# Group order, in-place weight rounding and queue choice in a one-core Strassen mixture-of-experts kernel

## The chip, the cores and the metric

The kernel runs on one core of one Trainium2 chip. The metric is the device time of one execution in microseconds. The median of three runs of the kernel before is 2360.71 us (2359.41 to 2364.94).

## What is computed

One token block `x` of 2048 rows and 512 columns goes through two branches, and a gate mixes them row by row:

```
g = sigmoid((x * gate_w).sum(-1))                      # one number per row
a = linear attention of x: 32 heads of 16, phi(t) = (t > 0 ? t + 1 : exp(t)) + 1e-6 on q and k,
    num = phi(q) @ (phi(k)^T v), den = phi(q) . sum(phi(k)), a = (num / den) @ wo
b = sum over 8 experts e of  softmax(x @ w_gate)[e] * (silu(x @ w1[e]) @ w2[e])   # all 8 chosen
out = g * a + (1 - g) * b
```

`w1[e]` is 512 x 1792 and `w2[e]` 1792 x 512. Everything is float32 in and out.

## The kernel before, in words

A float32 product is made of three passes on numbers rounded to the TensorE's 32-bit format: high x high, high x low, low x high (`mm3`, lines 57 to 60; `high` is a ScalarE copy that rounds, `low` a VectorE subtraction of what the rounding lost). All large products use a seven-product scheme on 2 x 2 blocks, so that each group of blocks has seven products P1 to P7, and sums and differences of blocks are made on VectorE.

The program is one order written out by hand, engine by engine, without a scheduler. It has two stages.

*Keys* (`keys`): projections for k, the gates' logits and `yT = x^T phi(k)`, and the running sum `pks` of phi(k), which GpSimd's queue adds up by 16 accumulating DMAs. At its very start four pieces of `x` and four of the weights `wk` are loaded in turn from SyncE's queue (SP); nine matmuls on zeros (`idle`) run on TensorE (PE) meanwhile. The last row tiles of this stage also prepare group 0 of the next (`prep(0, ...)`).

*Experts* (`experts`): a loop over ticks `u`. A *group* is a pair of hidden-column blocks: seven ticks, in six of which its first-layer ("up") products run, six matmuls of 128 x 512 per product; the seventh product runs in the second tick of the next group. `m.groups` is the order of the groups. Seven groups make one expert for one half of the rows (`X[h][e]`); two groups (`A[h]`, q = 0 and 1) make the attention queries of a half. The hidden activation of an expert group is one Silu on ScalarE (ACT); that of a query group is `phi`: Exp and Relu on ACT, one operation on VectorE (DVE), and a store to `pqd` by GpSimd's queue. Beside the products of group g, `prep(g + 1, step)` makes the operands of group g + 1 from raw weights (`rm`, loaded by `load(g + 2)` at the group's first tick): roundings on ACT, remainders and block sums on DVE. For groups of the first half (`both`) it also makes the second layer's weights, stores them to DRAM (`w2stash`, from tiles `ws`, and while `m.spare` is set, `wx`), and `load_w2` brings them back in pairs when they are needed. Query groups have no second layer in `prep`: it is lighter there.

The second-layer ("down") products start at u = 58 (`LAG`): from there each tick has one up product and one down product (`tick`). So the first 58 ticks have half the PE work per tick, and the same work on ACT, DVE and the DMA queues per group. In the kernel before, the query groups of the first half stand at places 0 and 4 of `m.groups`.

Small steps sit at fixed ticks: `state` (u = 5, the matmuls `kv`), `fold` (u = 7 to 10, matmuls `wp`), `normaliser` (u = 4, matmuls `z` that read `pks`), `gate_rows` (u = 65, two transposes into a bank of tag `a`, and 17 small stores that `load_wb` reads back at u = 74). PSUM banks: `a` two, `b` and `c` one each, `p` four for the down products. A group uses bank `a` for P1, for product 3 of the list, for product 5 and, in the next group, product 6; each of these waits until the step before has been read: by the copies on ACT (L663) or the additions on DVE (L668, L674). ACT, DVE and SP each work strictly in order.

At the end `columns(dt, ...)` transposes the last 512 rows, copies each of four column blocks out of PSUM in two halves and stores each half from SP; `dt` 2 and 3 in the last two ticks, 0 and 1 after the loop.

Of the kernel before, what the change touches and what calls it, by code (L numbers as in the profile page):

```python
# [11 lines left out]
F32R = mybir.dt.float32r  # L12
# [4 lines left out]
P = 128  # L17
# [7 lines left out]
TB = 512  # L25
NTB = S // TB
NTT = TB // P
# [3 lines left out]
G = (256, 266)  # L31
NPAIR = NF // 2
HALF = 2 * P
NHT = NT // 2
# [3 lines left out]
def f32(ap):  # L38
    return ap.bitcast(F32)


@with_exitstack
def gated_mix_kernel(ctx: ExitStack, tc: tile.TileContext, xT, x, wk, wv, wqkv_q, wo, wm, out):
    nc = tc.nc
    PS = bass.MemoryType.PSUM

    const = ctx.enter_context(tc.tile_pool(name="const", bufs=1))
    xpool = ctx.enter_context(tc.tile_pool(name="xpool", bufs=14))
    w1p = ctx.enter_context(tc.tile_pool(name="w1p", bufs=1))
    psum = ctx.enter_context(tc.tile_pool(name="psum", bufs=1, space=PS))  # L50
    dram = ctx.enter_context(tc.tile_pool(name="dram", bufs=1, space=bass.MemoryType.DRAM))
    ctx.enter_context(tc.manual_schedule())

    m = SimpleNamespace(nc=nc, tc=tc, const=const, xpool=xpool, w1p=w1p, psum=psum, v=nc.vector,
                        xT=xT, x=x, wk=wk, wv=wv, wq=wqkv_q, wo=wo, wm=wm, out=out)

    def mm3(ps, wh, wlo, xh, xl, start, stop):
        nc.tensor.matmul(ps, wh, xh, start=start, stop=False, skip_group_check=True)  # L58
        nc.tensor.matmul(ps, wh, xl, start=False, stop=False, skip_group_check=True)  # L59
        nc.tensor.matmul(ps, wlo, xh, start=False, stop=stop, skip_group_check=True)  # L60

    def act_copy(dst, src, scale=1.0, bias=0.0):
        nc.scalar.activation(dst, src, AF.Copy, scale=scale, bias=bias)  # L63

    def ps_tile(name, tag, bufs=None):
        return psum.tile([P, TB], F32, name=name, tag=tag, bufs=bufs or {"a": 2, "b": 1, "c": 1, "dn": 4}[tag])

    m.mm3, m.act_copy, m.ps_tile = mm3, act_copy, ps_tile


    def phi(dst, src):
        nc.scalar.activation(dst, src, AF.Exp)
        nc.scalar.activation(src, src, AF.Relu)
        nc.vector.scalar_tensor_tensor(dst, dst, 1.0, src, op0=ALU.min, op1=ALU.add)

    def eps_high(h, d):
        act_copy(h, d, bias=EPS)

    def eps_low(lo, d, h):
        nc.vector.scalar_tensor_tensor(lo, d, EPS, f32(h), op0=ALU.add, op1=ALU.subtract)  # L80

    m.phi, m.eps_high, m.eps_low = phi, eps_high, eps_low
    m.ident = const.tile([P, P], F32, name="ident")


    def x_tile(name, tag="x"):
        return xpool.tile([P, 2, TB], F32R, name=name, tag=tag, bufs=14 if tag == "x" else 2)

    m.x_tile = x_tile
    m.XO = [[None] * 7, [None] * 7]  # L90
    m.xstash = dram.tile([7, 2, P, 2 * TB], F32, name="xstash")
    m.w2stash = [dram.tile([P, 2, D], F32, name=f"w2stash{i}") for i in range(7 * (E * NPAIR + 2) // 2)]
    m.wgtd = dram.tile([E + 1, S], F32, name="wgtd")
    m.acct = dram.tile([2, 2, KT, P, TB], F32, name="acct")
    m.pqd = dram.tile([2, 2, KT, P, TB], F32, name="pqd")
    m.wpd = [dram.tile([P, D], F32, name=f"wpd{c}") for c in range(KT)]
    m.zcd = dram.tile([P, KT * 2 * NH], F32, name="zcd")
    m.spd = dram.tile([P, KT * P], F32, name="spd")

    X = [[SimpleNamespace(e=e, h=h, n=NPAIR) for e in range(E)] for h in range(2)]
    A = m.A = [SimpleNamespace(e=E, h=h, n=2) for h in range(2)]
    M = E // 2

    m.parts = [*X[0], *X[1][:M], A[0], *X[1][M:], A[1]]
    at = 0
    for part in m.parts:
        part.t0, at = at, at + 7 * part.n
    m.NTICK = at  # L110
    m.groups = [(part, q) for part in (*X[0], *X[1][:M], A[1], *X[1][M:]) for q in range(part.n)]

    m.groups.insert(0, (A[0], 0))
    m.groups.insert(4, (A[0], 1))
    m.NG = len(m.groups)
    for part in m.parts:
        part.gs = [g for g, (p, _) in enumerate(m.groups) if p is part]
    m.G1 = X[1][0].gs[0]

    m.beside = [*X[1][:2], *X[1][M:M + 2]]  # L120

    misc = ExitStack()
    m.misc = misc.enter_context(tc.tile_pool(name="misc", bufs=1, side="right"))


    def pad(pool):
        nc.gpsimd.memset(pool.tile([P, 24], F32, name="pad", tag="pad", bufs=1), 0.0)

    m.pad = pad
    weights(m)  # L130
    keys(m)
    experts(m, misc)

def weights(m):
# [50 lines left out]
    def prep(g, step):  # L187
# [25 lines left out]
        def low2(n, src, *prods):  # L213
            if both:
                w = ws.pop((g, n))
                v.tensor_sub(two(w, 1), src, f32(two(w, 0)))  # L216
                for half, prod in enumerate(prods):
                    stash(part, q, prod, w[:, :, half * HALF:(half + 1) * HALF])

        def block(i, j):  # L220
            return r[:, i, j] if both else r[:, i, j, 0]

        if step == 0:
            ops[g] = [None] * 7
            high(0, r[:, 0, :, 0], (0, 0), (2, HALF))
        elif step == 1:
            low(0, r[:, 0, :, 0])
            o = o_tile(f"o{g}_1", "oh", 2, HALF)
            act_copy(o[:, 0], r[:, 1, 1, 0])
            ops[g][6] = o, 0  # L230
            if both:
                act_copy(ws_tile(0)[:, 0, :HALF], r[:, 0, 0, 1])
            high2(1, r[:, :, 1, 1] if both else None)
        elif step == 2:
            o = ops[g][6][0]
            v.tensor_sub(o[:, 1], r[:, 1, 1, 0], f32(o[:, 0]))
            if both:
                w = ws.pop((g, 0))
                v.tensor_sub(w[:, 1, :HALF], r[:, 0, 0, 1], f32(w[:, 0, :HALF]))
                stash(part, q, "P1", w[:, :, :HALF])  # L240
        elif step == 3:
            low2(1, r[:, :, 1, 1] if both else None, "P2", "P4")
            v.tensor_add(block(1, 1), block(1, 0), block(1, 1))
            v.tensor_sub(block(1, 0), block(0, 0), block(1, 0))
        elif step == 4:
            v.tensor_sub(block(0, 0), block(1, 1), block(0, 0))
            v.tensor_sub(block(0, 1), block(0, 1), block(0, 0))
            high(2, r[:, 1, :, 0], (5, 0), (1, HALF))
        elif step == 5:
            low(5, r[:, 1, :, 0])  # L250
            high2(2, r[:, :, 0, 1] if both else None)
        elif step == 6:
            low2(2, r[:, :, 0, 1] if both else None, "P6", "P7")
            high(3, r[:, 0, :, 0], (3, 0), (4, HALF))
            high2(3, r[:, :, 1, 1] if both else None)
        else:
            low(3, r[:, 0, :, 0])
            low2(3, r[:, :, 1, 1] if both else None, "P3", "P5")
# [50 lines left out]
def keys(m):  # L309
# [76 lines left out]
    r1 = [hl_tile(f"r1{i}", F32) for i in range(2)]  # L386
    for k in range(KT):
        nc.sync.dma_start(x0[:, k, :], m.xT[0][:, k * TB:(k + 1) * TB])
        nc.sync.dma_start(r0[:, k, :], m.wk[:, k * G[0]:(k + 1) * G[0]])
    for i in range(2):  # L390
        at = KT * G[0] + 2 * i * G[1]
        nc.sync.dma_start(r1[i][:, :, :G[1]], m.wk[:, at:at + 2 * G[1]].rearrange("p (k f) -> p k f", k=2))
# [175 lines left out]
def experts(m, misc):  # L568
# [171 lines left out]

    w2s = {}

    ENDS = (NU + 12 - LAG) // 2

    def load_w2(i):
# [276 lines left out]
    def columns(dt, tag):  # L1022
        ps = ps_tile(f"oc{dt}", tag)
        for tt in range(NTT):
            nc.tensor.matmul(ps[:, tt * P:(tt + 1) * P], sums[1, dt, 1][:, tt * P:(tt + 1) * P], m.ident,
                             start=tt == 0, stop=True, is_transpose=True, skip_group_check=True)
        r = r_tile(f"oc{dt}")
        for i in range(2):
            c = slice(i * HALF, (i + 1) * HALF)
            if i and dt < 2:  # L1030
                v.tensor_copy(r[:, c], ps[:, c])
            else:
                act_copy(r[:, c], ps[:, c])
            at = (NHT + NTT + 2 * i) * P
            nc.sync.dma_start(m.out[at:at + 2 * P, dt * P:(dt + 1) * P].rearrange("(t p) d -> p t d", p=P),
                              r[:, c].rearrange("p (t d) -> p t d", d=P))


    AHEAD = {}
# [16 lines left out]

    drain()
    touch()
    loaded = highs = lows = 0
    ROWS0 = 105  # L1060
    for u in range(LAG + NTICK):
        n = u - LAG
# [52 lines left out]
            fold(u - 7)  # L1115
        if u in (0, 2, 59, 60, 62):
            gates((0, 2, 59, 60, 62).index(u))
        if u == 4:
            normaliser()
        if u == 65:  # L1120
            gate_rows()
        if u == 17:
            misc.close()
            m.w2p = ctx.enter_context(tc.tile_pool(name="w2p", bufs=1, side="right", reuse_waits="tile"))
        if u == 74:
# [3 lines left out]
        while loaded < END // 2 and loaded <= (n + (5 if u < NU + 8 else 9)) // 2:  # L1129
            load_w2(loaded)  # L1130
            loaded += 1
            if loaded == 3:
                m.pad(m.w2p)
        if g == m.G1 - 1 and k != 1:
            x_next(max(k - 1, 0))
        if g == m.G1 and k == 1:
# [56 lines left out]
```

## Time and profile before

| | |
|---|---|
| profiled execution | 2360.7 us, span 2359.0 us |
| median of three runs | 2360.71 us |
| PE busy | 2339.7 us (99%), 10492 matmuls |
| DVE busy | 1822.9 us (77%) |
| ACT busy | 1412.0 us (60%) |
| granted clock, mean | 0.998 |
| moved by DMA | 514.81 MB, mean 218 GB/s |

The span is what the trace covers; the execution's own time is 1.7 us more. Times below are microseconds from the span's start. In timeline rows the columns are start, duration, engine, line, operation, tiles, shape and count, and in brackets the engine's idle time just before and what ended it. A matmul's recorded duration overlaps the next one's.

### The profile page before, as it was taken

The page shows a single profiled execution, that of the slowest core. Times are in us where ns is not written, and L with a number is a line of the kernel's source. Part 1 is how long each engine was busy: PE and PEld are TensorE (multiplying, and loading weights), DVE is VectorE, ACT ScalarE, POOL GpSimd, SP SyncE. Part 2 cuts the span into 40 slices and gives each one's busy share as a digit, 9 for nine tenths or more (in the row PEclk, how much of TensorE's full clock was granted, in tenths as well). Part 3 has the DMA queues.
Part 4 walks back from the last instruction along what each step waited for, and adds up shares of the span by engine and source line. Part 5 has one row for each costly group of instructions (what it writes and reads, how often), then busy time and mean ns, then how long its engine had stood idle before and what let it go on. Part 6 is the DMA issues. An engine that isn't in the chain of part 4 may idle for free.

```text
span 2359.0 us, 31410 instructions
## 1 busy us (share of the span) xinstructions
PE 2339.7 (99%) x10492; PEld 1936.0 (82%) x10492; DVE 1822.9 (77%) x3103; ACT 1412.0 (60%) x2659; POOL 160.1 (7%) x222
## 2 busy tenths in 40 slices
PE   9999999999999999999999999999999999999998
PEld 8877888888888888888888888888888888888887
DVE  6788888888888888888677767776677777766666
ACT  6576666666666666666555555555565655555553
POOL 2101000000000000000000000000011000000101
PEclk9999999999999999999999999999999999999999
DMA  7778898888888898888845454654456645555566
GB/s 234 237 261 278 266 288 260 264 265 276 266 262 276 262 283 262 263 270 267 285 143 173 148 178 145 182 187 147 147 172 190 186 147 176 161 165 166 164 223 202
DMA packets 300593, 514.81 MB, mean 218 GB/s; under 512 B 24448, under 2 KB 195472, under 8 KB 300048
## 3 DMA queue, kind: packets, MB, share of 16 engines
q1 hardware_dynamic: 277088, 466.33, 59.6%
q0 software_dynamic: 23344, 46.49, 10.6%
q8 instruction: 82, 1.34, 0.2%
q14 instruction: 79, 0.65, 0.1%
HBM read 345.00 MB, written 163.52 MB: 216 GB/s over the span
## 4 chain that ended last, share of the span: by engine, by line
PE 93%; DVE 3%; DMA 2%; ACT 1%; issue 1%; SPq 0%; DVEq 0%; ACTq 0%
PE p L58 15%; PE p L60 15%; PE p L59 15%; PE a L58 8%; PE a L60 8%; PE a L59 8%; PE c L58 4%; PE c L60 4%; PE c L59 4%; PE b L60 2%; PE b L58 2%; PE b L59 2%; PE g L441 2%; DVE ho L738 1%; PE y L58 1%
## 5 line engine op out<-in xcount | busy, mean ns | idle before, releaser
L58 PE MATMUL p<-ho,w 128*128 128x512 f32 x1620 | 631.6, 390 | 1.8 <-ACT p L63 0.8
L60 PE MATMUL p<-ho,w 128*128 128x512 f32 x1620 | 630.3, 389 | 0.0
L59 PE MATMUL p<-ho,w 128*128 128x512 f32 x1620 | 630.3, 389 | 0.0
L738 DVE TENSOR_TENSOR ho<-s,ho 128x512 fp32r<-128x512 f32 x784 | 536.5, 685 | 47.8 <-ACT ho L63 45.9
L63 ACT ACTIVATE ho<-s 128x512 fp32r<-128x512 f32 x784 | 486.3, 621 | 14.0 <-PE p L60 8.0
L58 PEld LDWEIGHTS p<-ho,w 128*128 128x128 f32 x1620 | 304.1, 188 | 68.1 <-ACT p L63 2.9
L60 PEld LDWEIGHTS p<-ho,w 128*128 128x128 f32 x1620 | 304.1, 188 | 63.4
L59 PEld LDWEIGHTS p<-ho,w 128*128 128x128 f32 x1620 | 304.2, 188 | 62.9
L606 ACT ACTIVATE s<-s 128x512 f32<-128x512 f32 x224 | 141.3, 631 | 266.4 <-DVE s L668 198.8
L63 ACT ACTIVATE o<-rm 128x512 fp32r<-128x512 f32 x240 | 136.5, 569 | 83.5 <-PE a L60 60.8
L668 DVE TENSOR_TENSOR s<-c,s 128x512 f32<-128x512 f32 x116 | 80.1, 690 | 136.5 <-PE c L60 130.7
L63 ACT ACTIVATE o<-rs 128x512 fp32r<-128x512 f32 x224 | 127.3, 568 | 65.6 <-PE a L60 59.9
L63 ACT ACTIVATE ws<-rm 128x512 fp32r<-128x512 f32 x206 | 116.0, 571 | 64.9 <-DMA w2stash<-ws 56.3
L674 DVE TENSOR_TENSOR s<-a,s 128x512 f32<-128x512 f32 x116 | 80.0, 690 | 71.1 <-PE a L60 70.8
L606 ACT ACTIVATE s<-b 128x512 f32<-128x512 f32 x112 | 67.0, 599 | 113.3 <-PE b L60 100.9
L202 DVE TENSOR_TENSOR o<-rm,o 128x512 fp32r<-128x512 f32 x180 | 123.2, 685 | 3.9 <-ACT o L63 3.8
L63 ACT ACTIVATE s<-a 128x512 f32<-128x512 f32 x116 | 69.1, 596 | 90.7 <-PE a L60 89.8
L202 DVE TENSOR_TENSOR o<-rs,o 128x512 fp32r<-128x512 f32 x168 | 114.8, 683 | 7.7 <-ACT o L63 7.3
L216 DVE TENSOR_TENSOR ws<-rm,ws 128x512 fp32r<-128x512 f32 x156 | 106.8, 684 | 5.1 <-ACT ws L63 5.0
L63 ACT ACTIVATE s<-c 128x512 f32<-128x512 f32 x116 | 69.0, 595 | 25.6 <-PE c L60 25.6
L784 POOL DMA_DIRECT2D acct<-c x30 | 25.6, 852 | 801.4 <-DVE c L778 630.5
L63 ACT ACTIVATE b<-a 128x512 f32<-128x512 f32 x116 | 67.1, 579 | 21.4 <-PE a L60 21.1
(319 smaller groups left out, 4543.5 us busy)
## 6 DMA issues: line engine op xcount, KB each, us to landing
w<-w2stash SPq DMA_DIRECT2D x406, 512.0 KB, 4.0
w2stash<-ws SPq DMA_DIRECT2D x362, 256.0 KB, 4.3
rm<-wm SPq DMA_DIRECT2D x228, 256.0 KB, 5.1
rs<-wm SPq DMA_DIRECT2D x108, 256.0 KB, 4.0
wb<-wgtd SPq DMA_DIRECT2D x16, 512.0 KB, 5.3
w2stash<-wx SPq DMA_DIRECT2D x30, 256.0 KB, 4.2
acct<-c POOLq DMA_DIRECT2D x30, 256.0 KB, 5.4
acct<-d POOLq DMA_DIRECT2D x30, 256.0 KB, 5.4
```

Of the source, the lines that this page charges most:

```text
L58: nc.tensor.matmul(ps, wh, xh, start=start, stop=False, skip_group_check=True)
L59: nc.tensor.matmul(ps, wh, xl, start=False, stop=False, skip_group_check=True)
L60: nc.tensor.matmul(ps, wlo, xh, start=False, stop=stop, skip_group_check=True)
L63: nc.scalar.activation(dst, src, AF.Copy, scale=scale, bias=bias)
L202: v.tensor_sub(two(o, 1), src, f32(two(o, 0)))
L216: v.tensor_sub(two(w, 1), src, f32(two(w, 0)))
L441: nc.tensor.matmul(ps, xk((0, 0, 1)[j], tb, k, tt * P, (tt + 1) * P), gw[g][:, (0, 1, 0)[j], k, :], start=(k == 0 and j == 0), stop=(k == ...
L606: nc.scalar.activation(dst, src, AF.Silu)
L668: v.tensor_add(sn[g, 2], bank[g, "c"], sn[g, 2])
L674: v.tensor_add(sn[g, 3], bank[g, "a"], sn[g, 3])
L738: v.tensor_sub(h[1], s, f32(h[0]))
L784: nc.gpsimd.dma_start(m.acct[part.h, j, dt], s, accum_op=ALU.add)
```

## The change

Five edits. (1) The first half's two query groups are groups 0 and 1. (2) For the first six groups of the first expert the weights of P1 are rounded straight into the tiles from which the down products read them (`first_w2`), so they take no `ws` or `wx` tile and the first three `load_w2` fall away; the store to DRAM stays, since the second half reads it. For this the pool of those tiles opens at u = 7, not 17. (3) `normaliser` runs at u = 7, not 4, and `gate_rows` at u = 67, not 65. (4) At the start the four loads of `wk` are issued from ACT, those of `x` from SP. (5) At the end `columns` copies a whole block on ACT and stores it with one DMA for `dt` 0, 2 and 3; for `dt` 1 ACT and DVE copy a half each, and ACT and SP issue one store each.

```
-    m.groups = [(part, q) for part in (*X[0], *X[1][:M], A[1], *X[1][M:]) for q in range(part.n)]
-    m.groups.insert(0, (A[0], 0))
-    m.groups.insert(4, (A[0], 1))
+    m.groups = [(part, q) for part in (A[0], *X[0], *X[1][:M], A[1], *X[1][M:]) for q in range(part.n)]
...
+        begin = part is m.parts[0] and q < 6
+
+        def first(c):
+            return m.first_w2(q)[:, c] if begin else ws[g, 0][:, c, :HALF]
...
+            if both and not begin:
+                ws_tile(0)
             if both:
-                act_copy(ws_tile(0)[:, 0, :HALF], r[:, 0, 0, 1])
+                act_copy(first(0), r[:, 0, 0, 1])
...
-                w = ws.pop((g, 0))
-                v.tensor_sub(w[:, 1, :HALF], r[:, 0, 0, 1], f32(w[:, 0, :HALF]))
-                stash(part, q, "P1", w[:, :, :HALF])
+                v.tensor_sub(first(1), r[:, 0, 0, 1], f32(first(0)))
+                stash(part, q, "P1", m.first_w2(q) if begin else ws.pop((g, 0))[:, :, :HALF])
...
-        nc.sync.dma_start(r0[:, k, :], m.wk[:, k * G[0]:(k + 1) * G[0]])
+        nc.scalar.dma_start(r0[:, k, :], m.wk[:, k * G[0]:(k + 1) * G[0]])
...
+    def first_w2(q):
+        if q // 2 not in w2s:
+            w2s[q // 2] = m.w2p.tile([P, 2, 2, HALF], F32R, name=f"w2{q // 2}", tag="w2", bufs=3)
+            if q == 4:
+                m.pad(m.w2p)
+        return w2s[q // 2][:, q % 2]
...
-        for i in range(2):
+        at = (NHT + NTT) * P
+        rows = m.out[at:at + TB, dt * P:(dt + 1) * P].rearrange("(t p) d -> p t d", p=P)
+        if dt != 1:
+            act_copy(r, ps)
+            nc.sync.dma_start(rows, r.rearrange("p (t d) -> p t d", d=P))
+            return
+        for i, (copy, queue) in enumerate(((act_copy, nc.scalar), (v.tensor_copy, nc.sync))):
             c = slice(i * HALF, (i + 1) * HALF)
-            if i and dt < 2:
-                v.tensor_copy(r[:, c], ps[:, c])
-            else:
-                act_copy(r[:, c], ps[:, c])
-            at = (NHT + NTT + 2 * i) * P
-            nc.sync.dma_start(m.out[at:at + 2 * P, dt * P:(dt + 1) * P].rearrange("(t p) d -> p t d", p=P),
-                              r[:, c].rearrange("p (t d) -> p t d", d=P))
+            copy(r[:, c], ps[:, c])
+            queue.dma_start(rows[:, 2 * i:2 * i + 2], r[:, c].rearrange("p (t d) -> p t d", d=P))
...
-    loaded = highs = lows = 0
+    loaded, highs, lows = 3, 0, 0
...
-        if u == 4:
+        if u == 67:
+            gate_rows()
+        if u == 7:
             normaliser()
-        if u == 65:
-            gate_rows()
-        if u == 17:
             misc.close()
             m.w2p = ctx.enter_context(tc.tile_pool(name="w2p", bufs=1, side="right", reuse_waits="tile"))
...
-            if loaded == 3:
-                m.pad(m.w2p)
```

More of the change, by code (lines that the diff above doesn't have):

```diff
@@ L741, in experts @@
     w2s = {}
+    def first_w2(q):
[4 more added lines that the diff above has]
+        return w2s[q // 2][:, q % 2]
+    m.first_w2 = first_w2
     ENDS = (NU + 12 - LAG) // 2
```

## The prediction

> **What bounds the kernel now.** I read the page first, then a table of stretches, then who PE waited for, then the timeline at each of those waits.
>
> ```profile
> span 2359.0 us, 31410 instructions
> PE 2339.7 (99%) x10492; PEld 1936.0 (82%) x10492; DVE 1822.9 (77%) x3103; ACT 1412.0 (60%) x2659; POOL 160.1 (7%) x222
> ...
> 150.00:175.00 25.00, 21.17 (x84) 16.33 (x84) 19.33 (x32) 19.62 (x35) 2.28 (x5) 0.93 0.73 243
> 175.00:200.00 25.00, 22.57 (x97) 17.72 (x96) 21.54 (x37) 17.97 (x37) 0.00 (x0) 1.00 0.92 296
> 600.00:1130.00 530.00, 530.00 (x2340) 439.01 (x2339) 450.05 (x744) 340.62 (x643) 26.20 (x31) 1.00 0.87 268
> ...
> PE a L58 <- DVE s L674: 3.5, 2, 2.5
> PE z L870 <- DMA pks<-pk: 3.0, 1, 3.0
> PE wt L906 <- ACT s L606: 0.9, 1, 0.9
> ```
>
> PE is the bound: it idles 2359.0 - 2339.7 = 19.3 us of the span. Columns of the stretches: length, then PE, PEld, DVE, ACT, POOL busy, granted clock, DMA share, GB/s. In the long middle a matmul starts every 530 / 2340 = 0.226 us and nothing stands idle, so a tick's up product is 6 x 0.226 = 1.36 us. The change takes out no matmul; it can only take out idle and slow time at the start, around 97 to 220 us, and at the end. The rows of waits give us in total, times and longest. The idle lies in a few places: 25.00 - 21.17 = 3.8 and 25.00 - 22.57 = 2.4 between 150 and 200, 3.0 at `z`, the rest at the two ends.
>
> **The wait of `z` (edit 3).**
>
> ```profile
> 106.11 1.32 PE L870 MATMUL z<-ones,pks 128*128 128x32 f32 x8 [2.98 <-DMA pks<-pk]
> 107.24 0.77 PE L58 MATMUL c<-x11h,o 128*128 128x512 f32 x1
> 109.95 3.83 PE L854 MATMUL kv<-yT,wv 128*128 128x128 f32 x32
> 116.37 1.02 PE L861 MATMUL wp<-wo,kvt 128*128 128x512 f32 x2
> 106.11:109.95 3.84, 3.84 (x15) 3.26 (x16) 1.41 (x4) 0.00 (x0) 0.00 (x0) 0.58 1.06 390
> ...
> 98.85 7.12 DMA pks<-pk
> L840 SPq DMA_DIRECT2D wv<-wv x4: 340/443/928, 92.2 to 98.9; - x4
> L842 SPq DMA_DIRECT2D wo<-wo x4: 430/550/1191, 99.3 to 101.0; - x4
> ...
> wv<-wv SPq DMA_DIRECT2D x4, 256.0 KB, 5.1
> wo<-wo SPq DMA_DIRECT2D x4, 256.0 KB, 7.0
> ```
>
> PE stands 2.98 us because the last of the 16 additions to `pks` lands at 98.85 + 7.12 = 105.97. Behind the wait the granted clock is 0.58 until 109.95; in that time run `z` and the six matmuls of one up product, which last from the end of `z` (107.24, the start of its first matmul) to the start of `kv` (109.95): 2.71 us where 1.36 is usual. The price of the wait is 2.98 + 1.35 = 4.3 us.
>
> At u = 7 `z` comes after the products of u = 5, 6 and 7, `kv` and one `fold`. From 102.97 (106.11 - 2.98 is 103.13, less the 0.16 by which a matmul's record outlasts its slot): product to 104.33, `kv` (3.6) to 107.96, products to 110.7, `fold` 1.0, so `z` starts near 111.6, 5.6 us after `pks` has landed, and it is moved past no load on SP. What is late next: `kv` comes 5.6 us earlier and needs `wv`, whose last load was issued at 98.9 and lands 5.1 us later by the median, 104.0; `kv` starts at 104.3 and needs that quarter last, at 107. `fold` (two matmuls, 1.02) needs `wo` (issued by 101.0, 7.0 us, 108.0) at 110.7. Both are covered, by 2 to 3 us. DVE queues `zf` behind `z`: what waits behind it is a `low` for group 2, due 14 us later. The saving is 4.3; 3.5 if one of them comes late by a microsecond, 4.6 if `z` itself, too, ran slowly.
>
> **The second query group (edit 1).**
>
> ```profile
> 152.27 1.28 ACT L72 ACT_TABLE_LOAD   x1
> 155.73 0.50 PE L58 MATMUL a<-t5h,o 128*128 128x512 f32 x1 [0.29 <-ACT s L63]
> 157.22 0.69 DVE L668 TENSOR_TENSOR s<-c,s 128x512 f32<-128x512 f32 x1
> 161.22 0.70 PE L58 MATMUL a<-t6h,o 128*128 128x512 f32 x1 [2.48 <-DVE s L674]
> 161.22:165.65 4.43, 4.43 (x13) 3.50 (x13) 2.50 (x4) 3.81 (x8) 0.54 (x1) 0.61 0.75 261
> 170.95 0.50 PE L58 MATMUL a<-t5h,o 128*128 128x512 f32 x1 [1.06 <-ACT s L63]
> ```
>
> Here group 4 is a query group. Its sixth product may not touch bank `a` before DVE's L674 has read it, and on DVE L674 stands behind the `phi` of the block before: L668, Exp, Relu, `phi`'s DVE step, one `low`, L674. From the start of L668 to the matmul that is 161.22 - 157.22 = 4.0 us. Product 4 had ended by 155.73 - 0.29 = 155.44, so L668 ran 1.8 us late, after the Exp table load of 1.28. Price of the place: 0.29 + 2.48 idle, then 12 matmuls in 4.43 instead of 2.72 (clock 0.61), 1.7; and at 170.95, behind the return to the Silu table, 1.06. In all 5.5 us.
>
> In the changed kernel this group is number 1, behind another query group: no Exp load, and the load of the Silu table comes at u = 17. The chain of 4.0 us stays; L668 can start about 0.2 after product 4 (the 0.16 of a matmul's record, rounded up), and two products (2.72) lie between it and the matmul: a wait of 4.2 - 2.7 = 1.5 at u = 15. At u = 20 the wait of 1.06 comes again, and more: ACT and DVE lost the 1.7 us in which PE ran slowly and they caught up. How much of the 1.7 comes back as idle no row shows, between nothing (1.06) and all (2.8); I take 2.0, about half. So 3.5 remain and 2.0 are saved. At best (waits wholly covered by the four folds and `z` that now lie in group 1) 5.5 are saved; at worst the clock falls behind both waits, 2 x 1.7 more: 1.4 lost. The Trainium skill (TensorE: Matmul & The Clock Gate, section What's actually happening) halves the clock after at least one idle window of about 3.4 us; by that rule neither new wait would cost clock, and the trace differs, with half clock behind 2.48 us.
>
> **Weights rounded in place (edit 2).** Three loads of 512 KB fall away near 190 to 206, where DMA share is up to 0.99, and six `wx` tiles. PE idles 11.55 - 10.11 = 1.4 us in the group that starts at 182.00:
>
> ```profile
> 182.00:193.55 11.55, 10.11 (x43) 7.73 (x42) 8.98 (x15) 7.04 (x15) 0.00 (x0) 1.00 0.99 321
> 187.57 2.73 SPq L183 DMA_DIRECT2D w2stash<-ws  x3
> 190.48 0.38 SPq L754 DMA_DIRECT2D w<-w2stash  x1
> 193.46 0.63 ACT L63 ACTIVATE ws<-rm 128x512 fp32r<-128x512 f32 x1 [1.46 <-DMA w2stash<-ws]
> ```
>
> ACT stands there for a `ws` tile whose store is still out; this is the first expert's seventh group, which the edit leaves as it is, and the store was issued at 187.57, ahead of the first of the three loads (190.48). So I count 0, with 0.5 gained or lost as ends. The rounding itself takes the same operations.
>
> **`gate_rows` later (edit 3).** The row `PE wt` shows 0.9: the transposes need bank `a`, still being read from the tick before. At u = 67 that read is over: 0.9 saved, 0 if ACT is as late there.
>
> ```profile
> L913 POOL DMA_DIRECT2D wgtd<-wt x1: 507/507/507, 231.4 to 231.4; - x1
> ...
> DMA to landing us min/median/max: 2.5/4.1/5.4
> ...
> 243.35 0.33 SPq L772 DMA_DIRECT2D wb<-wgtd  x1
> ```
>
> Its 17 stores on GpSimd's queue move by two ticks, 4 x 1.36 = 5.4 us; the last, issued at 231.4, lands by 236.8 at the latest, so after the move by 242.2, and `load_wb` reads them at 243.35. A microsecond of cover stays; without it SP would hold its stores and loads back by as much, ahead of weights that are loaded two ticks early, so 0.
>
> **First loads and last stores (edits 4, 5).**
>
> ```profile
> 0.82 1.28 ACT L63 ACT_TABLE_LOAD   x1 [0.82 <-PEq L1185]
> 3.85 0.63 ACT L63 ACTIVATE x00h<-x 128x512 fp32r<-128x512 f32 x1 [1.75 <-DMA x<-xT]
> 1.28 0.42 SPq L389 DMA_DIRECT2D r<-wk  x1
> 6.92 1.21 PE L441 MATMUL g<-g,x00h 128*128 128x256 f32 x8 [0.38 <-ACT g L63]
> 8.90 1.21 PE L441 MATMUL g<-g,x01h 128*128 128x256 f32 x8 [0.18 <-ACT g L63]
> ...
> 2353.41 3.07 SPq L1035 DMA_DIRECT2D y<-oc  x6
> 2354.00:2355.00 1.00, 0.00 (x0) 0.00 (x0) 0.56 (x2) 0.05 (x1) 0.00 (x0) 1.00 1.00 318
> ```
>
> PE's idle at the start that loads can remove is 0.38 + 0.18 = 0.56. Four issues on ACT at 0.42 (SP's price; none from ACT is in the trace) push the table load from 0.82 to 2.5, its end to 3.8, just where `x` lands. I take 0.4 saved; ends 0.6 saved, 0.5 lost if an issue costs ACT more.
>
> At the end six issues at 0.5 become three on SP and one on ACT; by issue alone 1.4 us. But while they run the DMA engines are fully busy (share 1.00 from 2354 to 2355), and the bytes stay. I take 0.5; ends 1.4 saved and 0.4 lost. A rule that speaks against both edits: the Trainium skill (DMA: Bandwidth & Descriptors, section Issuing engines are not separate DMA queues) says that issuing from several engines saves only issue time. The busy share of the tail agrees with it.
>
> **The sum:** 0.4 + 4.3 + 2.0 + 0 + 0.9 + 0.5 = 8.1 us. The profiled execution took 2360.7, the median of the runs is the same: 2352.6.
>
> **Rivals.** *Two queues bring nothing.* Only the two middle gains and `gate_rows` stay: 7.2, so 2353.5. For: the full DMA engines of the tail. Chance 0.10.
>
> *Clock falls again.* The waits at u = 15 and 20 are near what cost clock before (2.48; 1.06 did not). Both with half clock: 2352.6 + 3.4 = 2356.0, about on the border of 0.2%. Chance 0.13.
>
> *The change doesn't do what it says.* `z` no longer waits, but `kv`, `fold` or group 2's operands do, by as much, since the loads of u = 0 and the `wv` and `wo` are all moved toward PE by 4 us with DMA share near 1: 2352.6 + 4.3 = 2356.9. Against: 2 to 3 us of cover. Chance 0.10.
>
> *Slower.* Groups 1 to 7 now all prepare full expert groups; before, a light one lay between.
>
> ```profile
> 172.44:182.00 9.56, 9.56 (x43) 7.85 (x42) 9.13 (x16) 7.66 (x16) 0.00 (x0) 1.00 0.91 287
> 137.59:147.11 9.52, 9.52 (x43) 7.88 (x42) 6.83 (x13) 6.42 (x13) 0.00 (x0) 1.00 0.82 262
> ```
>
> A full group needs 9.13 us of DVE in 9.56, a light one 6.83: nothing is left to catch up in, and raw weights land only as their group begins. If each of the six groups before the last paid what the group of 182.00 pays, 11.55 - 9.52 = 2.0, that is 12.2, and with one fall of the clock (1.7) 2366.5. It decides once a full group's DVE time passes 9.52. Against: the group of 172.44 runs without idle at 9.13. Chance 0.05.
>
> **How the numbers follow.** The forecast has 0.62. 0.2% is 4.7 us, about what a measurement tells from no change; the border is 2356.0. Faster: 0.62 + 0.10 + half of 0.13 = 0.79; same: the other half and 0.10, 0.16; slower 0.05. Low end: every term at its best, 0.6 + 4.6 + 5.5 + 0.5 + 0.9 + 1.4 = 13.5, 2347.2. High end: 2357.5, past the two cases near 2356 and 2357; the slow rival stays out.
>
> **What would show it.** Right: no idle before `z`, which stands after `wp`; PE idle of 1 to 2 us on DVE L674 at u = 15 and on ACT at u = 20, with the granted clock whole; about 1.4 us of idle, as before, while the first expert's seventh group is prepared; no idle at `wt`; the last store landing about 0.5 us closer behind the last transpose. Wrong: idle at `kv` or `wp`; half clock after 110; idle in every group between 140 and 185; a tail shorter by over 1 us.

## The result and the profile after

The changed kernel took 2351.48 us by the median of six runs (2350.17 to 2352.28); the kernel before took 2361.51 us on the same chip (six runs, 2357.91 to 2368.32). The ratio is 0.9954, 95% interval 0.9939 to 0.9969: 10.0 us faster, where 8.1 was forecast. The profiled execution, the shortest of the six, took 2350.17 us, 10.5 less than the one before it. Lines of code are those of the changed kernel from here on: L674 of before is now L678, L668 is L672, L870 is L883.

The head of the page, and the rows of who PE waited for (us in total, times, longest):

```profile
span 2348.5 us, 31397 instructions
PE 2335.1 (99%) x10492; PEld 1933.3 (82%) x10492; DVE 1820.5 (78%) x3102; ACT 1408.8 (60%) x2655; POOL 158.1 (7%) x222
...
PE a L58 <- ACT s L63: 2.6, 2, 1.9
PE a L58 <- DVE s L678: 2.0, 2, 1.4
```

PE's idle is 2348.5 - 2335.1 = 13.4 us where it was 19.3, and there is no row for `z` or `wt` any more. The span shrank by more than the 5.9 us of idle, mainly because PE also worked at half clock after two of the old waits, and that is booked as busy. So I compare when the same up products start:

```
first matmul of up tick   0        12       42       58       79       last matmul ends   span ends
before                 97.53   125.35   172.44   197.57   256.12      2353.62            2358.95
after                  96.65   119.64   164.45   189.13   246.53      2343.42            2348.47
gained on the way       0.88     4.83     2.28     0.45     1.15         0.61               0.28
```

The timeline of PE at the places of the prediction (start, duration, operation, and in brackets the idle before):

```profile
103.45 3.73 PE L867 MATMUL kv<-yT,wv 128*128 128x128 f32 x32
...
109.76 1.02 PE L874 MATMUL wp<-wo,kvt 128*128 128x512 f32 x2
110.61 0.97 PE L883 MATMUL z<-ones,pks 128*128 128x32 f32 x8
...
125.29 0.50 PE L58 MATMUL a<-t6h,o 128*128 128x512 f32 x1 [1.39 <-DVE s L678]
...
134.34 0.50 PE L58 MATMUL a<-t5h,o 128*128 128x512 f32 x1 [1.92 <-ACT s L63]
...
216.36 0.27 PE L919 MATMUL wt<-ident,gates 128*128 128x128 f32 x1
...
134.34:138.00 3.66, 3.66 (x16) 2.99 (x17) 3.64 (x7) 2.64 (x6) 0.00 (x0) 1.00 1.02 369
```

`kv`, `wp`, `z` and `wt` start with no idle before them. The second query group still waits twice, at u = 15 and u = 20, and the stretch behind the longer wait runs 16 matmuls in 3.66 us at clock 1.00 (the two columns after POOL's are the granted clock and the DMA share); before, the stretch behind the 2.48 ran 13 in 4.43 us at 0.61.

The two ends, as timeline rows:

```profile
0.82 1.87 ACTq L393 DMA_DIRECT2D r<-wk  x4
2.72 1.28 ACT L63 ACT_TABLE_LOAD   x1 [2.72 <-issue]
4.55 1.36 ACT L63 ACTIVATE x00h<-x 128x512 fp32r<-128x512 f32 x2 [0.55 <-DMA x<-xT]
5.24 1.22 PE L445 MATMUL g<-g,x00h 128*128 128x256 f32 x8
6.29 0.64 PE L445 MATMUL g<-g,x00l 128*128 128x256 f32 x4
6.78 1.12 PE L445 MATMUL g<-g,x00h 128*128 128x256 f32 x8
...
2341.95 1.47 PE L1038 MATMUL oc<-ident,tl 128*128 128x128 f32 x12
2343.26 0.98 SPq L1045 DMA_DIRECT2D y<-oc  x2
2344.03 0.40 ACTq L1050 DMA_DIRECT2D y<-oc  x1
2344.48 0.37 SPq L1050 DMA_DIRECT2D y<-oc  x1
2345.00:2346.00 1.00, 0.00 (x0) 0.00 (x0) 0.00 (x0) 0.00 (x0) 0.00 (x0) 0.99 0.97 285
```

At the start the two waits of `g` (0.38 and 0.18) are gone. At the end the last issue is over at 2344.48 + 0.37 = 2344.85, 1.43 us behind the last transpose (2.86 before), yet the span ends 5.05 us behind it (5.33 before). From 2345 to 2346 the DMA engines are busy 0.97 of the time although nothing is issued any more.

### The profile page after: what moved, and what is told of

The parts are those of the page before. It is cut to its first block, busy times and chain, and to the rows that moved or that the text cites. A ratio compares the mean times of both kernels' runs of the same rounds, so it can differ in the third digit from the quotient of the medians.

```text
span 2348.5 us, 31397 instructions
## 1 busy us (share of the span) xinstructions
PE 2335.1 (99%) x10492; PEld 1933.3 (82%) x10492; DVE 1820.5 (78%) x3102; ACT 1408.8 (60%) x2655; POOL 158.1 (7%) x222
## 4 chain that ended last, share of the span: by engine, by line
PE 96%; DVE 2%; ACT 1%; issue 1%; DMA 0%; SPq 0%; DVEq 0%; ACTq 0%
PE p L58 15%; PE p L60 15%; PE p L59 15%; PE a L58 9%; PE a L60 9%; PE a L59 9%; PE c L60 4%; PE c L58 4%; PE c L59 4%; PE b L60 2%; PE b L58 2%; PE b L59 2%; PE g L445 2%; PE y L58 1%; PE y L60 1%; PE y L59 1%
## 5 line engine op out<-in xcount | busy, mean ns | idle before, releaser
L672 DVE TENSOR_TENSOR s<-c,s 128x512 f32<-128x512 f32 x116 | 80.0, 690 | 133.3 <-PE c L60 129.2
L678 DVE TENSOR_TENSOR s<-a,s 128x512 f32<-128x512 f32 x116 | 80.0, 690 | 70.8 <-PE a L60 70.3
```

The costliest lines, as they stand in the source:

```text
L672: v.tensor_add(sn[g, 2], bank[g, "c"], sn[g, 2])
L678: v.tensor_add(sn[g, 3], bank[g, "a"], sn[g, 3])
```

## The experiments

Each was measured beside the kernel before on the same chip. The medians of before were 2361.04 for the first three experiments and the old loads and stores, 2362.02 for the three edits, the clock, the half stores and `gate_rows`, 2360.68 for the last two kernels. A tick's time below is that of the first matmul of its up product; where a figure is given for several kernels, each has one trace.

**The normaliser's place alone.** The kernel before, with

```
-        if u == 4:
+        if u == 7:
             normaliser()
```

> The kernel before with one change: normaliser at u = 7. Theory (each wait has its own price): the wait of z (2.98 us idle, then 1.35 us lost at the low clock) goes, some 4.5 us less, about 2356.2; the waits of the second query group stay as before (0.3 + 2.5 + 1.1 us idle, one stretch of low clock). Rival (the pause is needed): ACT, DVE and the DMA queues caught up in it, and the waits between 130 and 200 us grow by as much, so about 2360.5.

2354.97 us (2354.47 to 2355.58), ratio 0.9975 [0.9965, 0.9985]. Its tick 12 starts at 120.27, 22.99 after tick 0 (97.28); before, that took 27.82. The difference, 4.83, is what the whole change gains there. The second query group keeps both of its old prices:

```profile
156.15 0.78 PE L58 MATMUL a<-t6h,o 128*128 128x512 f32 x1 [2.43 <-DVE s L674]
165.97 0.50 PE L58 MATMUL a<-t5h,o 128*128 128x512 f32 x1 [1.15 <-ACT s L63]
156.15:160.00 3.85, 3.85 (x10) 3.09 (x11) 2.50 (x4) 3.14 (x7) 0.54 (x1) 0.56 0.74 254
```

Ten matmuls in 3.85 us at clock 0.56 behind the 2.43. The term of `z` is confirmed, as a whole and by itself. The medians differ by more, 6.1; in the traces 0.8 of the rest lies behind u = 79, where this edit does nothing.

**The groups' order alone.** The kernel before, with

```
-    m.groups = [(part, q) for part in (*X[0], ...
-    m.groups.insert(0, (A[0], 0))
-    m.groups.insert(4, (A[0], 1))
+    m.groups = [(part, q) for part in (A[0], *X[0], ...
```

> The kernel before with one change: both query groups of the first half in front. Theory: z still waits 3 us for pks and the clock falls; at u = 15 and 20 PE idles about 1.4 and 2.0 us at full clock in place of 0.3 + 2.5 + 1.1 us and a low clock, so 2 us less, about 2358.5. Rival (the order carries the whole gain, since an all-query start leaves the queues free): z's wait shrinks too, 5 us or more less, 2355.5 or below.

2355.26 us (ten runs, 2352.99 to 2364.39), ratio 0.9983 [0.9972, 0.9994]. Here my theory failed and its rival held. The wait of `z` at u = 4 was to stay, and in the profiled run it is gone. PE's row of `z`, the row of SP's loads of group 1's raw weights, and what the trace says of the last addition to `pks` (its issue, then issue to landing):

```profile
102.73 0.98 PE L868 MATMUL z<-ones,pks 128*128 128x32 f32 x8
87.18 4.45 SPq L167 DMA_DIRECT2D rm<-wq  x4
L459 POOL DMA_DIRECT2D pks<-pk x1: 852/852/852, 97.2 to 97.2; - x1
...
DMA to landing us min/median/max: 4.7/4.7/4.7
```

The last addition is issued at 97.2 and lands at 101.9, 0.8 ahead of `z`; before, it was issued at 98.85 and landed at 105.97. Group 1 is now a query group, and its raw load has no second-layer half: four loads of query weights instead of a full `rm`. So the order and the normaliser's place each remove this wait, and their gains don't add. With the old order the addition landed at 106.0 and 105.7 in two traces, with the new one between 101.9 and 105.3 in eight of ten. That the smaller load is why is likely, not shown. And the landing isn't firm. In the changed kernel's profiled run the same last addition went out much later:

```profile
L465 POOL DMA_DIRECT2D pks<-pk x1: 852/852/852, 103.3 to 103.3; - x1
...
DMA to landing us min/median/max: 7.1/7.1/7.1
```

It landed at 110.4, 0.2 us ahead of `z` at 110.61; in one more of the ten it landed as late, at 110.2. With the order alone `z` stands 102.73 - 97.29 = 5.44 us behind the start of tick 0. By that, as an estimate, `z` at u = 4 would have waited 8.3 us in the changed kernel's trace, 7.4 in the other late one, 0.3 to 2.9 in five and not at all in three. Three of the ten runs of the order alone took 2360.0 to 2364.4 us, the other seven 2353.0 to 2356.3; a late `pks` in those three would fit, but only one run was profiled.

**The changed kernel without the rounding in place.**

```
-        begin = part is m.parts[0] and q < 6
+        begin = False
...
-    loaded, highs, lows = 3, 0, 0
+    loaded, highs, lows = 0, 0, 0
... (and the pad of the pool behind the third load, as before)
```

> The changed kernel without the rounding in place: the six P1 weights go through wx tiles again and the first three loads of second-layer weights are back. Theory: 0 to 0.5 us more (2351.5 to 2352), all of it between u = 53 and 60. Rival (the three loads of 512 KB fall where the DMA engines are full and hold the stores of ws back): 2 us more or over, 2353.5 or above, as longer idle of PE between u = 54 and 60.

2352.68 us (2351.70 to 2353.24), ratio 0.9962 [0.9948, 0.9977], 1.2 us above the changed kernel's median: more than the 0 to 0.5 expected, less than the rival's 2. By the ticks, u = 58 to 65 takes 19.34 us, where the eight traces that keep the edit take 19.04 to 19.06; these 0.3 are the edit's worth. u = 49 to 58 takes 15.48 instead of 15.17, but five traces with the edit vary there from 14.72 to 15.23, and the run with the order alone, which lacks it too, takes 15.17; so that difference isn't firm. A further 1.59 us lies at u = 17 to 28, which the edit doesn't touch, and 0.47 before tick 0. The first of these is the clock:

```profile
134.81 0.50 PE L58 MATMUL a<-t5h,o 128*128 128x512 f32 x1 [1.92 <-ACT s L63]
132.12:135.54 3.42, 1.50 (x7) 0.94 (x6) 3.28 (x6) 2.10 (x4) 0.00 (x0) 1.00 0.91 282
135.54:138.95 3.41, 3.41 (x10) 2.63 (x9) 3.06 (x6) 2.66 (x5) 0.00 (x0) 0.50 1.07 375
```

The wait at u = 20 is 1.92 us, to the hundredth that of the changed kernel. There no low clock followed; here a stretch of exactly 3.41 us at 0.50 follows.

**When the clock falls.** To get many waits of many lengths, an extra matmul was put ahead of the second product in 24 later groups of the changed kernel, and it waits for 4 to 14 added copies on ScalarE:

```
+                if g >= 20 and g % 4 == 0 and g < 116:
+                    for _ in range(4 + 2 * (g // 4 % 6)):
+                        act_copy(m.late, bank[g - 1, "a"][:, :P])
+                    nc.tensor.matmul(bank[g, "c"][:, :P], m.late[:, :P], m.late[:, :P], start=True, stop=True)
```

> The changed kernel with 24 added waits of PE in the middle, one every four groups: 4, 6, 8, 10, 12 or 14 small copies on ACT (each 0.2 to 0.3 us) that one extra small matmul waits for, so idle of PE from about 1 to 3.5 us. Theory (fixed windows): the clock is judged in windows of 3.41 us on a grid that runs on through the execution; half clock follows for one window where more than half of a window, 1.7 to 1.9 us, was idle, so waits under 1.7 us never cost clock, waits of 2 to 3 us do or don't by their place on the grid. Rival 1 (length): one threshold between 2.0 and 2.4 us whatever the place. Rival 2 (a whole window): only waits of 3.4 us or more.

One run, 2519.63 us; the waits came out longer than meant, from 1.8 up to 9.8 us:

```profile
PE c L656 <- ACT late L63: 113.8, 24, 9.8
```

Every change of the granted clock in a trace lies on a grid of 3.413 us whose origin differs from run to run. Summing PE's idle in each grid window, over the traces of all kernels, from the first full clock to the last matmul:

```
window's clock   idle of PE in one grid window of 3.41 us       clock in the next window
1.00             up to 1.72 (the changed kernel's: 1.72)        1.00, always
1.00             1.77 to 1.92                                   1.00 four times, 0.50 three times
1.00             1.94 to 3.41, 28 windows                       0.50, always
0.50             up to 0.48                                     1.00, always
0.50             0.50 to 3.41, 13 windows                       0.50, always
```

So behind full clock a little over half a window of idle brings half clock, and a window that already runs at half clock needs far less idle for another one: 0.50 us was enough. Why the two differ no run here shows. Both rivals fall. A wait of 1.77 us inside one window was followed by half clock, and one of 3.42 that an edge at 2015.87 cut into 1.62 and 1.80 was not; nor was one of 2.39, cut into 0.75 and 1.64. The first two in the trace, each with the windows that tell:

```profile
1516.19 0.33 PE L656 MATMUL c<-late 128*128 128x128 f32 x1 [1.77 <-ACT late L63]
1517.53:1520.94 3.41, 3.41 (x9) 2.67 (x9) 3.38 (x7) 1.12 (x2) 0.00 (x0) 0.50 0.00 0
...
2017.67 0.33 PE L656 MATMUL c<-late 128*128 128x128 f32 x1 [3.42 <-ACT late L63]
2015.87:2019.29 3.42, 1.61 (x8) 1.37 (x9) 1.29 (x2) 1.65 (x6) 0.00 (x0) 1.00 0.28 108
2019.29:2022.70 3.41, 3.41 (x17) 2.83 (x16) 1.61 (x4) 1.41 (x3) 0.00 (x0) 1.00 0.03 12
```

The changed kernel's 1.92 us were cut by a grid edge at 134.15, into 1.72 and 0.2; the kernel without in-place rounding had all 1.92 inside one window (132.12 to 135.54, above). The changed kernel's two windows:

```profile
130.73:134.15 3.42, 1.70 (x8) 1.08 (x6) 3.28 (x7) 2.36 (x4) 0.65 (x2) 1.00 0.85 217
134.15:137.56 3.41, 3.22 (x14) 2.64 (x15) 3.39 (x6) 2.39 (x6) 0.00 (x0) 1.00 0.98 352
```

So a wait of 1.9 us costs 1.9 or about 3.5 by luck of the phase, and even 2.4 or 3.4 us of waiting can come without half clock where an edge falls near its middle.

**The changed kernel with the old loads at the start and the old stores at the end.**

```
-        nc.scalar.dma_start(r0[:, k, :], m.wk[:, k * G[0]:(k + 1) * G[0]])
+        nc.sync.dma_start(r0[:, k, :], m.wk[:, k * G[0]:(k + 1) * G[0]])
... (and columns as before)
```

> The changed kernel with the loads of wk from SP and the last stores as before. Theory: the start costs 0.9 us more (PE idles again at the second and third block of the first projection) and the end 0.3 us more: about 1.2 us more, 2352.7. The rival that two queues bring nothing: 0, 2351.5. The rival that issue time sets the end: 0.9 + 1.4 = 2.3 us more, 2353.8.

2352.05 us (2351.14 to 2352.71), ratio 0.9960 [0.9945, 0.9975]: 0.6 above the changed kernel, between the 1.2 expected and the first rival's 0, and less than the intervals can tell. In the traces tick 0 starts 1.04 later and the end takes 5.50 instead of 5.05. The 1.04 isn't all the edit's. Twelve traces, by loads and by the first record of full clock, that is, by where the grid lies:

```
old loads: clock from   4.34   6.00   6.35   7.59
           tick 0 at   97.53  97.28  97.29  97.69                                (mean 97.45)
new loads: clock from   4.44   4.79   5.36   5.42   5.83   6.57   6.77   6.80
           tick 0 at   96.65  96.71  96.92  96.75  97.11  97.25  97.34  97.34    (mean 97.01)
```

With the new loads PE depends on the clock's own start: eight `g` matmuls took 1.22 us in the changed kernel's profile (grid at 4.44) and 1.70 with the grid at 6.77, in a kernel with the same loads:

```profile
5.46 1.70 PE L445 MATMUL g<-g,x00h 128*128 128x256 f32 x8
```

The edit saves 0.9 when the clock comes early (97.53 against 96.65), and 0.04 to 0.17 when it comes at 6 to 6.6 (97.28 and 97.29 against 97.11 and 97.25). By the means it is 0.44, but the grid lies at other places in the two rows, so the mean worth stays rough.

**Half stores from two queues.** The changed kernel, with all eight last stores halved as before and issued by SP and ACT in turn.

```
+            (nc.scalar if i else nc.sync).dma_start(m.out[at:at + 2 * P, dt * P:(dt + 1) * P]...
```

> The changed kernel with the last stores in halves as before, but issued in turn from SP and ACT. Theory (the DMA engines set the end): the end comes 5.0 to 5.2 us after the last transpose, as with the changed kernel's whole blocks (5.05), though six issues are spread over two queues. Rival (issue time): 4.3 us or less, as the last issue ends over 1 us earlier than before.

One run, 2353.43 us. From the last matmul to the end of the span it takes 5.72 us, where 5.0 to 5.2 was expected and 4.3 by the rival: more than the old stores from one queue (5.33 to 5.50 in four traces) and than the new ones (5.03 to 5.07 in six, 5.34 in a seventh). It can't decide between the two, though, because the issues didn't come earlier. ACT issues and copies in one order, its last copy waited for DVE's, and its last issue ended 2.92 us behind the last matmul (2346.00), as late as the 2.86 of before:

```profile
2347.66 0.38 ACT L63 ACTIVATE oc<-oc 128x256 f32<-128x256 f32 x1 [0.92 <-DVE oc L1044]
2348.54 0.38 ACTq L1048 DMA_DIRECT2D y<-oc  x1
...
2347.00:2348.00 1.00, 0.00 (x0) 0.00 (x0) 0.21 (x1) 0.34 (x1) 0.00 (x0) 1.00 0.98 280
```

What tells is the changed kernel itself. Its last issue ends 1.43 us earlier than before, but its last store takes 3.1 us from issue to landing instead of 1.9. It lands 4.15 us behind the last matmul, as in all seven traces with the new stores (4.14 to 4.16); the old ones land at 4.30 to 4.33 in four traces. So 1.43 us less of issue brought 0.17, while the engines were busy 0.97 of the time at 285 GB/s: they, and not the issues, hold the end. A further 0.89 to 1.21 us pass from the last landing to the end of the span, with old and new stores alike, and that part makes the difference of the spans larger or smaller than 0.17.

**`gate_rows` back at u = 65.** The changed kernel, with

```
-        if u == 67:
+        if u == 65:
             gate_rows()
```

> The changed kernel with gate_rows at u = 65 as before. Theory: PE waits 0.9 us again at the transposes, and nothing else moves; u = 65 to 68 takes 1.1 us more. Rival (the wait was there because of what lay before): none, 0.

One run, 2352.6 us. My theory failed, its rival held: no wait for `wt` comes back, and u = 65 to 79 takes only 0.25 us longer.

```profile
212.35 0.39 PE L60 MATMUL p<-ho,w 128*128 128x512 f32 x1
212.80 0.30 PE L919 MATMUL wt<-ident,gates 128*128 128x128 f32 x1
```

The rest of its distance to the changed kernel is half clock behind u = 20 (1.57 by the ticks u = 17 to 28) and 0.51 behind u = 79. In the run with the order alone, which has neither the later `gate_rows` nor the rounding in place, the wait for `wt` is 1.0; without the rounding in place but with the later `gate_rows` it is 0. So either of the two seems to be enough. The run with the order alone differs in the place of `z`, the first loads and the last stores as well, so this isn't shown edit by edit.

**Three edits against the waits that were left.** (a) In the first query group `phi`'s DVE step stands behind the addition of s3, (b) in the second the copy of s2 stands ahead of its tick's roundings, (c) the early roundings use the second address until u = 54 in place of 50.

```
+            if g == 1:                        # (a), behind v.tensor_add(sn[g, 3], ...)
+                v.scalar_tensor_tensor(dst, dst, 1.0, sn[g, 2], op0=ALU.min, op1=ALU.add)
...
+            act_copy(sn[g, 2], bank[g, "a"])  # (b), k == 4
+            if g == 2:
+                other()
...
-        m.spare = ho_tile if u < LAG - 8 else None
+        m.spare = ho_tile if u < LAG - 4 else None
```

> The changed kernel with its three remaining waits of PE taken on: in query group 1 the DVE step of phi stands behind L678's addition; in group 2 the copy out of bank a stands ahead of that tick's roundings on ACT; and the P1, P2/P4 weights of the seventh group go through the wx tiles (m.spare until u = 54, not 50). Theory: idle of 1.4 at u = 15 and 1.9 at u = 20 goes to under 0.5 each, the 2.0 between u = 54 and 57 to under 1.0; 4 us less in all, 2347.5, and the clock no longer hangs on the phase. Rival (ACT and DVE are full in groups 1 to 7 and PE waits for them somewhere): the waits move to the next ticks, 2350 to 2351.5.

2346.69 us (2346.29 to 2347.69), ratio 0.9927 [0.9908, 0.9946]. (a) takes the whole wait at u = 15: u = 12 to 15 is 1.55 shorter. (c) ends three waits at u = 49 to 56, and that stretch is 2.64 shorter. The stretch from the start of u = 49 to that of u = 58, in the changed kernel and in this one:

```profile
173.97:189.13 15.16, 13.12 (x55) 9.90 (x54) 12.24 (x21) 10.93 (x22) 0.00 (x0) 1.00 0.83 266
173.47:186.00 12.53, 12.53 (x56) 10.06 (x55) 12.10 (x21) 11.21 (x23) 0.00 (x0) 1.00 1.00 328
```

The idle there, 15.16 - 13.12 = 2.04, is gone. (b) shortened its wait from 1.92 to 0.65 but a new one of 1.4 came two ticks on. The last two runs ask about it.

**Without (b)** (only a and c):

> The kernel after the change with two of the three edits of the best version so far: in the first query group the VectorE step of phi on s2 behind the addition of s3, and the part sums of the first roundings to a second address until u = 54 in place of 50. The copy of s2 in the second query group stays behind its tick's roundings. Theory (that copy only moved a wait: the 1.9 us at u = 20 became 0.65 there and 1.37 at u = 22): 2346.5 to 2348.5, the wait at u = 20 back at 1.9 us and the one at u = 22 gone, which leaves the sum of waits in that group within 0.3 us; where a half clock follows the 1.9 us wait, 1.6 us more. Rival (the copy was worth its whole wait): 2348.5 to 2350.

2348.06 us (2346.94 to 2348.95), ratio 0.9939 [0.9920, 0.9957]: inside the range that was expected.

**With (b), and the additions of s2 and s3 in the second query group ahead of their ticks' block sums and differences:**

```
+            v.tensor_add(sn[g, 2], bank[g, "c"], sn[g, 2])   # k == 5; the same for s3, k == 6
+            if g == 2:
+                other()
```

> All three edits, and besides in the second query group the additions of s2 and s3 (u = 21 and 22) ahead of their ticks' block sums and differences on VectorE. Theory (the wait of 1.37 us at u = 22 comes from the order on VectorE, which has 0.8 us of 9.41 us free in the stretch before): the wait goes, about 1.2 us less than with the three edits alone, 2345.5. Rival (VectorE is full in that stretch, and what is put behind the additions is late in its turn): the differences of u = 22 and 23 come late instead, a wait of 1 to 2 us at u = 23 or 24 for an operand, 2346.5 to 2348.

2346.40 us (2345.83 to 2347.15), ratio 0.9932 [0.9912, 0.9952]. PE's waits between 97 and 200 us, three kernels: with all three edits, without (b), and with the additions ahead:

```profile
PE a L58 <- DVE s L686: 1.4, 1, 1.4
PE a L58 <- ACT s L63: 0.6, 1, 0.6
```

```profile
PE a L58 <- ACT s L63: 2.3, 1, 2.3
```

```profile
PE a L58 <- DVE s L690: 0.7, 1, 0.7
PE a L58 <- ACT s L63: 0.6, 1, 0.6
```

In all, 2.0, 2.3 and 1.4 us. (b) alone moves the wait, and the intervals with and without it overlap; what it buys is that no single wait is long enough for half clock, which followed the 2.3 (of which 1.94 lay in one window). Neither forecast for the last kernel was right: the wait halved, and no other took its place. In the kernel with all three edits, DVE carries 8.91 us in the 9.70 us that hold both waits:

```profile
126.90:136.60 9.70, 7.71 (x32) 5.48 (x30) 8.91 (x16) 7.72 (x15) 1.21 (x3) 1.00 0.82 251
```

The version with all three edits and the one with the additions ahead, which can't be told apart here, beat the changed kernel by about 5 us (by medians) and the kernel before by about 15.

## Why the prediction was right, and where its steps were not

The total came out right, 10.0 where 8.1 was forecast, and so did the main mechanism, a wait of `z` with half clock behind it. Two things in the profiled run were luck: the clock stayed full behind u = 20, and 0.61 us belongs to no edit.

**The wait of `z`: 4.3 forecast, 4.83 measured, right.** The price (idle plus half clock) was read rightly, and `kv` and `fold`, the next to be late, were covered. The slow part was a little short: the window of half clock lasts 3.41 us, which costs 1.7, and 1.35 was counted. The margin was to be 5.6 us behind the landing of `pks`. It was 5.6 with the normaliser's place alone, but 0.2 in the changed kernel's trace and 1.2 in one more; in the other seven with `z` at u = 7 it was 5.6 to 9.5. And the gain was booked to edit 3 alone, while the order by itself takes the wait away too in its profiled run and, by their times, perhaps in seven of its ten.

**The second query group: 2.0 forecast, 2.28 in the profiled run, by luck of the phase.** Waits of 1.5 at u = 15 and 2.0 at u = 20 were forecast; 1.39 and 1.92 came, on the forecast engines and lines. The step that doesn't hold is that the clock stays whole behind them. It isn't a matter of the wait being short of 2.48, but of whether 1.8 to 1.9 us of it fall into one window of the grid. Seven traces run this group as the changed kernel does. From u = 12 to 42 two of them take 44.79 and 44.81 us and five, with half clock behind u = 20, take 46.34 to 46.39; before it was 47.09. So the gain is 2.3 or 0.7. The rival of the falling clock (0.13) was true in five of the seven, behind one wait and not both.

**Rounding in place: 0 forecast, 0.3 measured,** inside the ends that I had given. It lies at u = 58 to 65. While the first expert's seventh group is prepared, PE was to idle 1.4 as before; it idled 0.75 + 0.69 there and 0.60 in a third wait just behind, which my stretch had cut off. That third wait was 1.0 before and lies between 0.25 and 0.71 in seven traces of the new order, 0.47 with the order alone, so what it lost isn't this edit's. That these waits hang on the tiles which take the roundings is what (c) suggests: the three kernels that have it lose all three waits. It was never run without (a).

**`gate_rows`: 0.9 forecast, wait gone, but the reason is only a part.** The segment gained 1.15. Undoing the edit costs 0.25. The step that failed is "0 if ACT is as late there": I compared ACT at u = 67 with ACT at u = 65 before, and not with ACT at u = 65 after the other edits.

**First loads: 0.4 forecast, 0.88 in the two profiled runs,** 0.44 by the rough means over twelve traces, with single pairs from 0.04 to 0.88. My bound of 0.56 (the rows' idle) was no bound: matmuls that run on a clock not yet granted are booked as busy.

**Last stores: 0.5 forecast, 0.28 in the spans, 0.17 by the landings.** The engines, not the issues, set the end, as the busy share had said: of the 1.43 us of issue time saved I had let 0.5 through, and 0.17 came. The Trainium skill (DMA: Bandwidth & Descriptors, section Issuing engines are not separate DMA queues) has issuing from several engines save only the time of issue. The changed kernel's trace agrees, with 1.43 saved there and 0.17 at the landing.

**The rest.** 0.61 between u = 79 and the last matmul belongs to no edit: the other traces without added copies vary there by 0.7 us (2096.7 to 2097.4), and 0.34 of it is one wait for a second-layer weight at 1158 in the kernel before, which three others have too. The rival of two useless queues isn't ruled out by the times: with the old loads and stores the kernel was 0.6 slower, within the intervals. Late operands of `kv`, `fold` or group 2 did not show; and of the seven full groups only the one that already paid before did pay.

## What to carry to other kernels

Price a wait with the slow clock behind it, and shorten or split one that is near 1.9 us even where it can't be removed: the same wait cost 1.9 or 3.5. What counts is the idle inside one window of the clock's grid, and one profile shows only one place of that grid. When two edits each remove the same wait, the gain counts once, so ask of each edit what the wait would be with the others already made. Where an engine is nearly full, reordering it moves a wait; moving a step that nobody waits for (a), or giving a tile a second address (c), removed one.

## What the runs showed of the hardware

The granted clock is decided on windows of 3.413 us on a grid that starts elsewhere in each run (first full clock between 4.34 and 7.59 us). Behind a window at full clock, at least 1.94 us of PE's idle in it gave half clock in the next in 28 of 28 cases, up to 1.72 never. Behind a window at half clock, 0.50 us or more gave another in 13 of 13, up to 0.48 never. The Trainium skill (TensorE: Matmul & The Clock Gate, section What's actually happening) gives the same free-running window of 3413 ns, and the cold clock after at least one idle window. The window's length agrees; the "idle window" is here, at full clock, one with little over half of it idle.

The chain of 16 accumulating DMAs to `pks` is not steady: over the twelve traces its last link was issued between 96.8 and 103.3 us and took 4.4 to 7.5 us to land. A DMA issue took ACT 1.87 / 4 = 0.47 us at the start and 0.40 at the end.
